# Attention and gated convolution on one core: key loads of later batches over 17 to 22 groups, later expected landings and a new set of order weights

## The chip, the cores and the metric

The kernel runs on one core of a Trainium2 chip. A time is device microseconds (us) from start to end of one execution of the program. The core has a matrix engine (PE, with its weight loads shown apart as PEld), a vector engine (DVE), a scalar engine (ACT), a general engine (POOL) and a queue engine (SP), which here issues every DMA: loads, stores and DMA transposes. Each engine works through its own instructions strictly in the order in which they stand in the program, and waits for semaphores of the others.

## The reference, cut to what matters

```python
# B, C, Hh, Ww = 4, 128, 384, 32;  N = Hh * Ww = 12288 queries a batch;  r = 4
kv_pool = kv.reshape(B, H // r, r, W // r, r, C).mean(axis=(2, 4))
k = v = kv_pool.reshape(B, -1, C) @ w_sr             # 768 keys a batch
s = (q @ k.transpose(0, 2, 1)) / np.sqrt(C)
a = np.exp(s - s.max(-1, keepdims=True))
a /= a.sum(-1, keepdims=True) + 1e-09
x = a @ v                                            # (B, 12288, 128)
gate_pre[t] = sum(conv_w[k] * x[t - 4 + k] for k in range(5))
gate = 1.0 / (1.0 + np.exp(-gate_pre))
out = (gate * (x @ w_val)) @ w_out
```

## The kernel before, in words

**Tiles.** Queries are worked in groups of 512 (98 groups over all four batches: 24 each, the last 512 queries in three smaller ones). A group has four parts j of 128 queries. For each part PE makes scores (line 527: six matmuls into one of three PSUM buffers `s`), DVE takes the row maximum (`nm`, line 539), ACT the exponential (line 546), DVE the factor one over the row sum (`r`, lines 555 and 560), ACT writes the scaled rows as the high half in f16 (`hl`, line 574), DVE the low half (`hl`, line 585), which also gives the PSUM buffer back. Two parts share one `hl` buffer, and when both are written SP turns them with one DMA transpose (`pt`, line 598). So a group has two transposes; below they are called its first and its second. When both have landed PE multiplies them with the values (`av`, line 669, 18 matmuls), ACT copies the result to `x`, POOL works the five taps of the gate (lines 730 and 738), and PE, DVE and ACT do the two projections (lines 757, 761, 766, 771). Every second group SP loads `q` for two groups (512 KB, line 499) and stores `out` for two groups (512 KB, line 794).

**Keys.** The keys and values of a batch come from 16 pieces of `in_kv` of 384 KB each. SP loads a piece into one of six buffers `kvt` (line 283), and DVE sums it in two halves into `pool` (`TENSOR_REDUCE`, line 301). When all 16 are summed PE projects them (line 354), ACT and DVE split them into high and low, and PE makes the values (line 447). The pieces of batch 0 come at the start of the program. Those of batch 1, 2 and 3 are loaded and summed while the groups of the batch ahead run.

**What sets the order.** Nothing here is ordered by hand. The code first adds all steps to a `Plan` with an engine, an assumed duration, a due time and what they follow; `Plan.order` then runs a list scheduler over them with buffers, and the instructions are written out in the order that it finds. The due times of the steps are the group's place times `PERIOD` plus an offset from the table `DUE`; among the steps that an engine can begin within `WAIT` of the first one the scheduler takes the one that is due first. For a DMA it keeps a queue of its own, in which a transfer lands `DMA_LEAD`, its duration and `DMA_TAIL` after its issue, and `CLUMP` pulls copies together. These assumed times change only the order of instructions. Each engine then waits for real events on the chip.

The loads of the later batches have a first time, rounded up to every second group by `grid`:

```python
at = (lambda i: 0.0) if first else (lambda i: grid((b * NG - 22 + i // 2 * 2) * T))
s = plan.add("SP", 1.0 if first else 1.3, due(-20 * T + i) if first else at(i), run,
             takes=(buf,), start=at(i))
```

So piece 0 and 1 are meant for one stretch of two groups, piece 2 and 3 for the next, and so on: two pieces for every two groups, over 16 groups, from 22 groups ahead of the batch to 6 ahead of it. Below, two groups with their loads are called a slot.

Of the kernel before, what the change touches and what calls it, by code (L numbers as in the profile page):

```python
# [19 lines left out]
PIECES = 16  # L20
PARTS = 2

PERIOD = 10.07
DUE = dict(keys=-41.48, vals=-22.35, vals0=16.98, q=-57.56, qh=-1.25, ql=-98.01,
           score=(-8.15, -7.91, -7.36, -6.79), max=(-32.5, -0.27, -16.2, -12.23),
           exp=(5.15, -44.96, 24.96, -21.92), hi=(-25.76, -32.45, 4.7, -5.26),
           lo=(20.43, -7.54, 6.54, -13.12), turn=(-0.19, 7.8, 7.04, -30.79), pe=-16.02, thi=48.8,
           tlo=0.37, r=(-26.97, -87.57, -32.65, -35.38), grid=-0.27, av=20.43, avs=3.47,
           halo=41.12, x=41.54, gate=30.15, th=62.39, val=46.47, h=-8.22, out=4.34, evac=7.73,
           store=61.44, end_diag=-62.42, end_gate=17.3, end_th=63.48, end_val=94.9, end_h=-18.98,  # L30
           end_out=45.64, end_evac=-44.23)


class Step:
# [8 lines left out]
class Plan:  # L43
# [2 lines left out]

    EDGE = 0.04
    LAG = dict(PE=0.16, ACT=0.1, DVE=0.085, POOL=0.04, SP=0.0)
    WAIT = dict(PE=0.08, ACT=0.2, DVE=0.11, POOL=0.01, SP=0.59)
    DMA_LEAD, DMA_TAIL, CLUMP = 1.3, 0.8, 39.63  # L50

    def __init__(self):
        self.steps, self.stock = [], {}
# [14 lines left out]
    def order(self):  # L68
# [10 lines left out]
        dma = 0.0  # L79
        until, placed = {}, []  # L80
        while any(ready.values()):
            best = None
            for e, items in ready.items():
# [8 lines left out]
                if not ests:  # L92
                    continue
                t0 = min(t for t, _ in ests)
                s = min((s.due - (s.kind == last[e] == "copy") * self.CLUMP, n, s)
                        for n, (t, s) in enumerate(ests) if t <= t0 + self.WAIT[e])[2]
# [4 lines left out]
            t, e, s = best  # L101
# [6 lines left out]
            if e == "SP":  # L108
                copy = s.kind == "copy"
                free[e] = t + (0.5 if copy else s.dur)  # L110
                switch = 1.0 if last[e] == "copy" and not copy else 0.0
                dma = max(dma + switch, t + self.DMA_LEAD) + s.dur
                s.end = dma + self.DMA_TAIL
            else:
                free[e] = t + s.dur
                s.end = t + s.dur + s.lag
# [33 lines left out]
def attn_moe_kernel(ctx, tc, qT, kvT, w_sr, w_moe, outT):  # L150
# [9 lines left out]
    NG = N // GQ  # L160
# [3 lines left out]
    T = PERIOD  # L164
# [100 lines left out]
    def grid(t):  # L265
        return D["grid"] + 2 * T * -(-(t - D["grid"]) // (2 * T))

    def setup(b, st):

        first = b == 0  # L270
        due = (lambda at: at - 40.0) if first else (lambda at: b * NG * T + at)
        at = (lambda i: 0.0) if first else (lambda i: grid((b * NG - 22 + i // 2 * 2) * T))
        sums = {}
        holder = {}

        def load(i):
            buf = "o" if first and i in SPARE else "kvt"
            cuts = (0, PC * RR // 2, PC * RR) if first and i == PIECES - 1 else (0, PC * RR)

            def run():  # L280
                s.tile = tile_of(s, buf)
                for c0, c1 in zip(cuts, cuts[1:]):
                    nc.sync.dma_start(out=s.tile[:, c0:c1], in_=kvT[b, i, :, c0:c1])  # L283
            s = plan.add("SP", 1.0 if first else 1.3, due(-20 * T + i) if first else at(i), run,
                         takes=(buf,), start=at(i))
            return s, buf

        def pool_of(s, k0):
# [194 lines left out]
    def group(g, prev, nxt):  # L483
# [9 lines left out]
        if off == 0 or g.i == 1:  # L493
            cols = GQ if g.i < 2 else 2 * GQ

            def load():
                if off == 0:
# [2 lines left out]
                                  in_=qT[g.b, :, g.c0:g.c0 + cols])  # L500
            at = FIRST_Q[g.i] if g.i in FIRST_Q else grid(t0 + D["q"])
            ld = plan.add("SP", 1.6 * cols / (2 * GQ), at, load, [ld],
                          takes=("q",) if off == 0 else (), start=at)
            if off == 0:
                g.io.ld = ld

# [59 lines left out]
        def straight(j, sc, r):  # L566
# [28 lines left out]
            def turn():  # L595
                if g.pt_by is s_t:
# [4 lines left out]
            s_t = plan.add("SP", 1.40 * width, t0 + j * T / 4 + D["turn"][j], turn,  # L601
                           [s_lo] if alone else [s_lo, g.los[j - 1]],
                           takes=() if g.pt_by else ("pt",),
                           frees=[(g.hl_by, "hl")], kind="turn")
            owner(s_t)
            g.ready.append(s_t)

# [245 lines left out]

ON_PE, IN_S = 2, 4
TAIL, LAST, LAST_TURNED = 4, (2, 1, 1), ((), (0,), (0,))
FIRST_VALS = 26.0
FIRST_Q = {0: 17.0, 1: 17.5, 2: 18.0, 4: 26.0}
SPARE, FOLDED = (6, 7, 8), (3, 5, 8, 10, 12)
TURNED = ((),)
# [28 lines left out]
```

## Time and profile before

| | us |
|---|---|
| median of 3 runs | 1046.62 |
| lowest and highest of them | 1041.93 and 1050.76 |
| the profiled execution | 1049.91 |
| its span, first to last instruction | 1048.0 |
| PE busy in it | 1001.0 |
| DVE, ACT, POOL busy in it | 929.9, 886.2, 931.3 |
| mean granted clock of PE | 0.987 of full |

The profiled execution is 3.3 us above the median and lies 1.9 us above its own span. A span of 1048.0 us over 98 groups mixes three kinds of time: the start, before the first groups run, stretches in which keys of the next batch are loaded beside the groups, and stretches without key loads. They have to be read apart.

### The profile page before, as it was taken

Reading aid. Unit: us, or ns where it says so; the run is one execution under the profiler, and the core shown is the slowest. Engines: PE = TensorE matmul, PEld = TensorE weight load, DVE = VectorE, ACT = ScalarE, POOL = GpSimd, SP = SyncE. Lnnn points to the kernel's source line nnn. Section 1 sums busy time; section 2 is a strip of 40 time slices with the busy share of each in tenths; the row PEclk is TensorE's granted clock in tenths of the full one; section 3 lists DMA queues with packets and bytes.
Section 4 is the critical chain, followed back from the end, with each engine's and each line's share of the span. In section 5 each row is a group of like instructions: output and inputs, shape, how many; then the busy total and the mean of one; then the engine's idle time right before and its main releaser. Section 6 shows DMA issues by size and latency. Waiting matters only on the chain.

```text
span 1048.0 us, 15461 instructions
## 1 busy us (share of the span) xinstructions
PE 1001.0 (96%) x4586; PEld 612.0 (58%) x4586; DVE 929.9 (89%) x1806; ACT 886.2 (85%) x1584; POOL 931.3 (89%) x1069
## 2 busy tenths in 40 slices
PE   4789999999999999999999999999999999999998
PEld 3555555556665555556666555555566666666655
DVE  6799989989899998989989999899998988988884
ACT  1688878889888888879998888798999899989884
POOL 5179989998999988989899999899999999999994
PEclk9799999999999999999999999999999999999999
DMA  8599999999999999999999999999999999999983
GB/s 313 135 220 231 222 220 242 235 226 209 218 213 226 228 236 248 214 225 208 217 209 218 249 242 222 230 236 220 224 214 197 222 201 217 214 202 212 191 171 91
DMA packets 616994, 227.05 MB, mean 217 GB/s; under 512 B 595536, under 2 KB 596304, under 8 KB 616912
## 3 DMA queue, kind: packets, MB, share of 16 engines
q1 hardware_dynamic: 616912, 226.07, 102.4%
q8 instruction: 37, 0.61, 0.2%
q14 instruction: 45, 0.37, 0.1%
HBM read 50.66 MB, written 25.17 MB: 72 GB/s over the span
## 4 chain that ended last, share of the span: by engine, by line
PE 82%; DMA 9%; DVE 6%; SPq 1%; issue 1%; ACT 1%; POOL 0%; ACTq 0%
PE s L527 35%; PE av L669 31%; PE m L757 7%; PE m L766 7%; DMA kvt<-in_kv 4%; DMA pt<-hl 4%; DVE hl L585 3%; DVE nm L539 2%; DVE pool L301 1%; DMA o<-in_kv 1%; SPq L598 1%; ACT hl L574 0%; PE m L354 0%; SPq L283 0%; PE m L447 0%
## 5 line engine op out<-in xcount | busy, mean ns | idle before, releaser
L738 POOL TENSOR_TENSOR gate<-gate,tap 128x512 f32<-128x512 f32 x376 | 482.2, 1282 | 9.8
L585 DVE SCALAR_TENSOR_TENSOR hl<-s,r,hl 128x768 f16<-128x768 f32 x382 | 386.1, 1013 | 38.0 <-ACT hl L574 37.5
L669 PE MATMUL av<-pt,vh 128*128 128x512 f16 (+2 forms) x1176 | 385.8, 379 | 3.1 <-DMA pt<-hl 3.1
L546 ACT ACTIVATE s<-s,nm 128x768 f32<-128x768 f32 x384 | 336.6, 877 | 55.3 <-DVE nm L539 54.6
L539 DVE TENSOR_REDUCE nm<-s 128x1 f32<-128x768 f32 x384 | 362.8, 946 | 14.4 <-PE s L527 13.9
L574 ACT ACTIVATE hl<-s,r 128x768 f16<-128x768 f32 x382 | 338.3, 906 | 41.7 <-DVE r L560 36.5
L527 PE MATMUL s<-kh,qh 128*128 128x512 f32 (+1 forms) x768 | 267.5, 429 | 26.2 <-DVE r L555 17.2
L730 POOL TENSOR_SCALAR tap<-x,wb 128x512 f32<-128x512 f32 x376 | 254.5, 698 | 0.0
L669 PE MATMUL av<-pt,vl 128*128 128x512 f16 (+2 forms) x588 | 222.2, 378 | 0.0
L527 PEld LDWEIGHTS s<-kh,qh 128*128 128x128 f32 x768 | 135.1, 191 | 144.3 <-issue 59.9
L669 PEld LDWEIGHTS <-vh 128*128 128x128 f16 x1176 | 113.8, 98 | 154.2 <-issue 59.9
L527 PE MATMUL s<-kl,qh 128*128 128x512 f32 (+1 forms) x768 | 199.9, 342 | 0.0
L527 PE MATMUL s<-kh,ql 128*128 128x512 f32 (+1 forms) x768 | 199.2, 341 | 0.0
L513 POOL TENSOR_TENSOR ql<-q,qh 128x512 fp32r<-128x512 f32 (+1 forms) x98 | 123.2, 1257 | 24.5 <-ACT qh L509 24.5
L527 PEld LDWEIGHTS s<-kh,ql 128*128 128x128 f32 x768 | 120.0, 192 | 17.3
L527 PEld LDWEIGHTS s<-kl,qh 128*128 128x128 f32 x768 | 119.6, 191 | 17.6 <-DVE kl L394 0.2
L730 POOL TENSOR_SCALAR gate<-x,wb 128x512 f32<-128x512 f32 x94 | 65.5, 697 | 59.4 <-ACT x L687 58.4
L766 PE MATMUL m<-h,wm 128*128 128x512 f32 x188 | 100.4, 616 | 0.0
L757 PE MATMUL m<-x,wb 128*128 128x512 f32 x188 | 96.0, 592 | 0.0
L669 PEld LDWEIGHTS <-vl 128*128 128x128 f16 x588 | 58.3, 99 | 62.0 <-issue 24.4
L301 DVE TENSOR_REDUCE pool<-kvt 128x24 f32<-128x384 f32 x114 | 60.4, 540 | 21.8 <-DMA kvt<-in_kv 21.8
L771 ACT ACTIVATE o<-m 128x512 f32<-128x512 f32 x94 | 56.3, 599 | 23.0 <-PE m L766 22.3
(67 smaller groups left out, 622.8 us busy)
## 6 DMA issues: line engine op xcount, KB each, us to landing
q<-in_q SPq DMA_DIRECT2D x47, 512.0 KB, 5.6
out<-o SPq DMA_DIRECT2D x47, 512.0 KB, 3.3
kvt<-in_kv SPq DMA_DIRECT2D x60, 384.0 KB, 4.3
pt<-hl SPq DMA_TRANSPOSE x191, 6.3
o<-in_kv SPq DMA_DIRECT2D x3, 384.0 KB, 8.0
q<-in_q SPq DMA_DIRECT2D x2, 256.0 KB, 5.2
kvt<-in_kv SPq DMA_DIRECT2D x2, 192.0 KB, 4.5
raw<-in_w_moe SPq DMA_DIRECT2D x1, 261.0 KB, 2.9
```

The costliest lines, as they stand in the source:

```text
L301: v.tensor_reduce(out=dst, in_=src[:, part * n:][:, :n], axis=AX.X, op=ALU.add)
L513: nc.gpsimd.tensor_tensor(out=g.ql, in0=g.io.q[:, mine], in1=g.qh.bitcast(F32), op=ALU.subtract)
L527: nc.tensor.matmul(t[:, c0:c1], a[:, sl], k[:, c0:c1], start=(i == 0), stop=(i == 2))
L539: v.tensor_reduce(out=s.tile, in_=sc.tile[:, :NK], axis=AX.X, op=ALU.max, negate=True)
L546: nc.scalar.activation(out=sc.tile[:, :NK], in_=sc.tile[:, :NK], func=AF.Exp, bias=mx.tile, accum_out=sc.tile[:, NK:NK + 1])
L574: nc.scalar.activation(out=g.hls[j // 2][:, half, 0], in_=sc.tile[:, :NK], func=AF.Copy, scale=r.tile)
L585: v.scalar_tensor_tensor(out=hl[:, half, 1], in0=sc.tile[:, :NK], scalar=r.tile, in1=hl[:, half, 0], op0=ALU.mult, op1=ALU.subtract)
L669: nc.tensor.matmul(g.av, st[name][:, k * P:(k + 1) * P], g.pt[:, :, a * NCH + k], start=(i == 0), stop=(i == len(AV) - 1))
L730: nc.gpsimd.tensor_scalar(out=s.tile, in0=src(k), scalar1=wt(k), scalar2=1.0, op0=ALU.mult, op1=ALU.mult)
L738: nc.gpsimd.tensor_tensor(out=g.gate, in0=g.gate, in1=tap.tile, op=ALU.add)
L757: nc.tensor.matmul(g.m, st["wb"][:, :C], g.x[:, HALO:], start=True, stop=True)
L766: nc.tensor.matmul(g.m2, wout, g.h, start=True, stop=True)
```

## The change

It does four things, all in the planner's input. The pieces of a later batch get first times spread evenly from 27 groups ahead of the batch (22 for batch 1, whose pieces cannot be asked for before the program begins) up to `KEYS_BY`, 5 groups ahead of it. The scheduler adds `SLACK` to the assumed landing of a key load (2.0 us), a query load (0.5 us) and a transpose (0.1 us). `PERIOD` and the whole table `DUE` have other numbers, of which two lines are shown. `WAIT` and `CLUMP` have other numbers. No instruction is added, removed or resized; the first lines of the file grow, so that a line of the kernel before has a number higher by 6 to 8 after (283 becomes 289, 301 becomes 307, 598 becomes 605).

```diff
-PERIOD = 10.07
-DUE = dict(keys=-41.48, vals=-22.35, vals0=16.98, q=-57.56, qh=-1.25, ql=-98.01,
+PERIOD = 9.97
+DUE = dict(keys=-39.58, vals=-35.42, vals0=17.37, q=-44.21, qh=4.86, ql=-80.97,
...
+SLACK = dict(keys=2.0, q=0.5, turn=0.1)
...
-    WAIT = dict(PE=0.08, ACT=0.2, DVE=0.11, POOL=0.01, SP=0.59)
-    DMA_LEAD, DMA_TAIL, CLUMP = 1.3, 0.8, 39.63
+    WAIT = dict(PE=0.07, ACT=0.26, DVE=0.12, POOL=0.07, SP=0.8)
+    DMA_LEAD, DMA_TAIL, CLUMP = 1.3, 0.8, 16.23
...
-                s.end = dma + self.DMA_TAIL
+                s.end = dma + self.DMA_TAIL + s.lag
...
-        at = (lambda i: 0.0) if first else (lambda i: grid((b * NG - 22 + i // 2 * 2) * T))
+        lo = -22 if b == 1 else -27
+        at = (lambda i: 0.0) if first else (
+            lambda i: grid((b * NG + lo + (KEYS_BY - lo) * i / PIECES) * T))
...
-                         takes=(buf,), start=at(i))
+                         takes=(buf,), start=at(i), lag=0.0 if first else SLACK["keys"])
...
+                          lag=0.0 if g.i in FIRST_Q else SLACK["q"])
...
+                           lag=SLACK["turn"])
...
-FIRST_VALS = 26.0
+FIRST_VALS, KEYS_BY = 26.0, -5
```

What this does to the order shows best on the queue of SP. Here is a stretch of it in the middle of batch 1, before, while the pieces of batch 2 come in. `kvt` is a key piece, `q` a query load, `out` a store, and a `DMA_TRANSPOSE` is half a group; two transposes with one `pt` are one group:

```order
L598 DMA_TRANSPOSE pt_4058<-hl_3974 128x24x128
L283 DMA kvt_4092<-in_kv 128x768
L283 DMA kvt_4096<-in_kv 128x768
L499 DMA q_4109<-in_q 128x1024
L598 DMA_TRANSPOSE pt_4058<-hl_4052 128x24x128
L794 DMA out<-o_3996 128x1024
L598 DMA_TRANSPOSE pt_4172<-hl_4131 128x24x128
L598 DMA_TRANSPOSE pt_4172<-hl_4185 128x24x128
L598 DMA_TRANSPOSE pt_4322<-hl_4225 128x24x128
L283 DMA kvt_4353<-in_kv 128x768
L283 DMA kvt_4360<-in_kv 128x768
L499 DMA q_4374<-in_q 128x1024
```

And the same stretch after:

```order
L605 DMA_TRANSPOSE pt_4196<-hl_4137 128x24x128
L802 DMA out<-o_4010 128x1024
L289 DMA kvt_4240<-in_kv 128x768
L505 DMA q_4255<-in_q 128x1024
L605 DMA_TRANSPOSE pt_4196<-hl_4191 128x24x128
L605 DMA_TRANSPOSE pt_4318<-hl_4234 128x24x128
L605 DMA_TRANSPOSE pt_4318<-hl_4313 128x24x128
L605 DMA_TRANSPOSE pt_4436<-hl_4383 128x24x128
L802 DMA out<-o_4257 128x1024
L289 DMA kvt_4485<-in_kv 128x768
L289 DMA kvt_4500<-in_kv 128x768
L505 DMA q_4507<-in_q 128x1024
```

A slot now holds one piece or two: for batch 2 and for batch 3 five slots of two and six of one, eleven in all, where there were eight of two. For batch 1 seven slots of two remain, and the last two pieces stand in slots of their own. The store now stands ahead of the pieces and of the group's second transpose; before it stood behind that transpose.

On DVE the first sum of a piece moves. Before, in the same batch, the sum of piece 6 (`kvt_4092`) stands between the two low halves of the next group's first transpose, with 14 instructions between it and the low half that the transpose ahead of the loads waits for:

```order
L539 TENSOR_REDUCE nm_4127<-s_4102 128x1
L555 SCALAR_TENSOR_TENSOR r_4136<-s_4080,unit 128x1
L560 RECIPROCAL r_4140<-r_4136 128x1
L585 SCALAR_TENSOR_TENSOR hl_4131<-s_4063,r_4124,hl_4131 128x768
L301 TENSOR_REDUCE pool_3412<-kvt_4092 128x24
L585 SCALAR_TENSOR_TENSOR hl_4131<-s_4080,r_4140,hl_4131 128x768
L555 SCALAR_TENSOR_TENSOR r_4170<-s_4102,unit 128x1
```

After, the sum of piece 10 (`kvt_4240`) stands half a group later, with 24 instructions between it and that low half (`hl_4137`):

```order
L592 SCALAR_TENSOR_TENSOR hl_4234<-s_4221,r_4286,hl_4234 128x768
L562 SCALAR_TENSOR_TENSOR r_4316<-s_4272,unit 128x1
L567 RECIPROCAL r_4327<-r_4316 128x1
L307 TENSOR_REDUCE pool_2794<-kvt_4240 128x24
L592 SCALAR_TENSOR_TENSOR hl_4313<-s_4248,r_4303,hl_4313 128x768
L546 TENSOR_REDUCE nm_4338<-s_4320 128x1
L592 SCALAR_TENSOR_TENSOR hl_4313<-s_4272,r_4327,hl_4313 128x768
```

At the start SP's queue begins with the loads of `q` for the first groups (`q_179` is groups 0 and 1, in two halves). Before:

```order
L499 DMA q_179<-in_q 128x512
L499 DMA q_186<-in_q 128x1024
L499 DMA q_179<-in_q 128x512
L499 DMA q_210<-in_q 128x1024
L499 DMA q_258<-in_q 128x1024
L598 DMA_TRANSPOSE pt_280<-hl_260 128x24x128
L598 DMA_TRANSPOSE pt_280<-hl_296 128x24x128
L283 DMA kvt_374<-in_kv 128x768
L283 DMA kvt_379<-in_kv 128x768
L499 DMA q_392<-in_q 128x1024
L598 DMA_TRANSPOSE pt_412<-hl_361 128x24x128
L598 DMA_TRANSPOSE pt_412<-hl_400 128x24x128
```

After, the second half of `q_179` stands behind one more load, and the first transpose of group 2 (`pt_366`) stands ahead of both transposes of group 1 (`pt_422`):

```order
L505 DMA q_179<-in_q 128x512
L505 DMA q_186<-in_q 128x1024
L505 DMA q_196<-in_q 128x1024
L505 DMA q_179<-in_q 128x512
L505 DMA q_258<-in_q 128x1024
L605 DMA_TRANSPOSE pt_280<-hl_260 128x24x128
L605 DMA_TRANSPOSE pt_280<-hl_292 128x24x128
L605 DMA_TRANSPOSE pt_366<-hl_325 128x24x128
L289 DMA kvt_396<-in_kv 128x768
L289 DMA kvt_398<-in_kv 128x768
L505 DMA q_412<-in_q 128x1024
L605 DMA_TRANSPOSE pt_422<-hl_388 128x24x128
```

From the middle of batch 3 on, where no keys are left to load, PE, DVE, ACT and POOL hold the same order as before within a group, but for one `av` matmul that PE takes ahead of a score instead of behind it; on SP the query load stands one or two transposes earlier.

## Rows read from the trace of the kernel before

**Rows 1.** The page's first part: busy us of each engine, share of the span, instructions.

```profile
PE 1001.0 (96%) x4586; PEld 612.0 (58%) x4586; DVE 929.9 (89%) x1806; ACT 886.2 (85%) x1584; POOL 931.3 (89%) x1069
```

**Rows 2.** Busy time by stretch. Columns: the stretch and its length, then busy us (and instructions) of PE, PEld, DVE, ACT and POOL, the granted clock, the share of the DMA engines, GB/s. The stretches are the start; the rest of batch 0, in which the keys of batch 1 come in; batch 1, with the keys of batch 2; batch 2, with those of batch 3; batch 3 up to its last groups, without key loads.

```profile
0.00:60.00 60.00, 37.60 (x148) 28.36 (x148) 43.43 (x93) 28.72 (x52) 20.52 (x37) 0.89 0.76 221
60.00:275.00 215.00, 207.27 (x952) 124.53 (x952) 198.01 (x386) 187.66 (x337) 198.30 (x227) 0.99 1.09 226
275.00:531.00 256.00, 248.19 (x1125) 148.90 (x1124) 231.31 (x452) 221.13 (x395) 234.66 (x265) 0.99 1.08 222
531.00:781.00 250.00, 244.53 (x1119) 147.35 (x1119) 229.86 (x447) 220.45 (x394) 233.20 (x265) 0.99 1.09 228
781.00:1010.00 229.00, 229.00 (x1058) 141.79 (x1057) 204.49 (x391) 207.44 (x370) 221.92 (x251) 1.00 1.01 205
```

**Rows 3.** The same view for four short stretches in which the granted clock fell.

```profile
136.00:146.00 10.00, 7.89 (x29) 3.96 (x27) 6.81 (x14) 6.01 (x12) 7.07 (x8) 0.83 1.13 266
408.00:420.00 12.00, 9.79 (x38) 5.36 (x36) 7.72 (x16) 7.53 (x13) 8.24 (x10) 0.86 1.15 260
452.00:464.00 12.00, 9.89 (x38) 5.24 (x37) 7.79 (x16) 7.62 (x14) 8.63 (x11) 0.86 1.11 255
661.00:672.00 11.00, 8.56 (x35) 5.17 (x33) 6.62 (x15) 6.87 (x13) 6.15 (x6) 0.84 1.07 271
```

**Rows 4.** Pieces of the chain that ended last, in order of time: start us, us, what. The first three lie in batch 1 while keys are loaded, the last two in batch 3.

```profile
320.98 4.13 DMA kvt<-in_kv
...
344.30 10.03 DMA pt<-hl
...
406.67 4.29 DMA kvt<-in_kv
...
830.09 1.31 PE av L669 x6
...
909.91 1.31 PE av L669 x6
```

**Rows 5.** DVE's instructions in order of time in one slot of batch 1: start us, us, engine, line, operation; in brackets idle time before it and what ended it.

```profile
357.50 1.00 DVE L585 SCALAR_TENSOR_TENSOR hl<-s,r,hl 128x768 f16<-128x768 f32 x1
...
362.90 0.68 DVE L761 SCALAR_TENSOR_TENSOR h<-th,m 128x512 f32<-128x512 f32 x1
363.49 0.15 DVE L555 SCALAR_TENSOR_TENSOR r<-s,unit 128x1 f32<-128x1 f32 x1
...
363.75 0.94 DVE L539 TENSOR_REDUCE nm<-s 128x1 f32<-128x768 f32 x1
...
364.88 1.02 DVE L585 SCALAR_TENSOR_TENSOR hl<-s,r,hl 128x768 f16<-128x768 f32 x1
368.06 0.55 DVE L301 TENSOR_REDUCE pool<-kvt 128x24 f32<-128x384 f32 x1 [2.17 <-DMA kvt<-in_kv]
```

**Rows 6.** The sums of key pieces (line 301) by stretch, 62 to 275, 275 to 531 and 531 to 781 us. For the first the group with its durations in ns; then for each what DVE waited for ahead of them: us in all, times.

```profile
L301 DVE TENSOR_REDUCE pool<-kvt x29: 531/534/553, 62.5 to 213.0; 128x24 f32<-128x384 f32 x29
...
  DMA kvt<-in_kv: 4.8, 4
...
  DMA kvt<-in_kv: 8.5, 5
...
  DMA kvt<-in_kv: 5.7, 4
```

**Rows 7.** SP's instructions in order of time in one slot of batch 1. For a row of several the us run from the first one's start to the last one's end.

```profile
364.05 1.06 SPq L283 DMA_DIRECT2D kvt<-in_kv  x2
...
365.69 6.52 SPq L598 DMA_TRANSPOSE pt<-hl  x1
372.30 0.53 SPq L794 DMA_DIRECT2D out<-o  x1
372.93 12.42 SPq L598 DMA_TRANSPOSE pt<-hl  x3
385.40 1.05 SPq L283 DMA_DIRECT2D kvt<-in_kv  x2
```

**Rows 8.** The same in batch 3, without key loads.

```profile
801.25 13.28 SPq L598 DMA_TRANSPOSE pt<-hl  x3
814.58 0.58 SPq L794 DMA_DIRECT2D out<-o  x1
815.54 9.02 SPq L598 DMA_TRANSPOSE pt<-hl  x2
824.66 0.53 SPq L499 DMA_DIRECT2D q<-in_q  x1
```

**Rows 9.** Transposes on SP by stretch, issue durations in ns (least, median, most), and us from issue to landing (the same three): the one that stands behind two pieces at 344.3 us, then 780 to 1005 us.

```profile
DMA to landing us min/median/max: 10.0/10.0/10.0
...
L598 SPq DMA_TRANSPOSE pt<-hl x45: 3073/4074/4887, 781.0 to 1000.6; - x45
...
DMA to landing us min/median/max: 4.6/6.3/7.9
```

**Rows 10.** PE's first `av` matmul of group 74, in order of time.

```profile
828.22 0.38 PE L669 MATMUL av<-pt,vh 128*128 128x512 f16 x1
```

**Rows 11.** Two instructions of the start in order of time: ACT's copy of the second half of `q_179`, and PE's first `av` matmul of group 1.

```profile
33.45 0.62 ACT L509 CAST qh<-q 128x512 fp32r<-128x512 f32 x1 [1.59 <-issue]
...
60.41 0.38 PE L669 MATMUL av<-pt,vh 128*128 128x512 f16 x1 [0.35 <-DMA pt<-hl]
```

More of the change, by code (lines that the diff above doesn't have):

```diff
@@ L21 @@
 PARTS = 2
-PERIOD = 10.07
-DUE = dict(keys=-41.48, vals=-22.35, vals0=16.98, q=-57.56, qh=-1.25, ql=-98.01,
[L25 to L31, printed above, removed]
+PERIOD = 9.97
+DUE = dict(keys=-39.58, vals=-35.42, vals0=17.37, q=-44.21, qh=4.86, ql=-80.97,
+           score=(-7.47, -6.32, -5.63, -6.47), max=(-23.77, -6.1, 13.1, -11.57),
+           exp=(0.09, -30.82, -8.74, -13.77), hi=(-29.44, -20.58, 0.7, -43.56),
+           lo=(22.34, -32.12, 5.51, 24.31), turn=(-11.32, 15.47, 2.1, 15.6), pe=6.0, thi=29.07,
+           tlo=-11.13, r=(-50.81, -28.34, -47.73, -28.55), grid=-1.12, av=20.41, avs=4.86,
+           halo=63.51, x=42.45, gate=30.41, th=53.25, val=47.33, h=-3.27, out=11.86, evac=21.59,
+           store=52.32, end_diag=-56.57, end_gate=26.44, end_th=54.36, end_val=54.8, end_h=-26.7,
+           end_out=56.32, end_evac=-38.92)
+SLACK = dict(keys=2.0, q=0.5, turn=0.1)
 class Step:
@@ L502, in group @@
             ld = plan.add("SP", 1.6 * cols / (2 * GQ), at, load, [ld],
-                          takes=("q",) if off == 0 else (), start=at)
+                          takes=("q",) if off == 0 else (), start=at,
+                          lag=0.0 if g.i in FIRST_Q else SLACK["q"])
             if off == 0:
@@ L603, in straight @@
                            takes=() if g.pt_by else ("pt",),
-                           frees=[(g.hl_by, "hl")], kind="turn")
+                           frees=[(g.hl_by, "hl")], kind="turn",
+                           lag=SLACK["turn"])
             owner(s_t)
```

## The prediction

> **What bounds the kernel now.** I read the busy times first, then the stretches, then the chain, then the two queues that it names. The page has PE at 96% [rows 1], which alone says little about where time can still come from. The stretches say it [rows 2]: in batch 3, where no keys are loaded, PE is busy for 229.00 of 229 us, so nothing on another engine can shorten that part while PE's work stays what it is. In the three stretches with key loads PE is idle for 7.73, 7.81 and 5.47 us (length less busy), 21.0 in all, and in 22.4 us of the start. Besides, the granted clock drops to its half level (1.2 instead of 2.4 GHz) for short times, each where PE has just waited [rows 3]: (1 - 0.83) x 10, (1 - 0.86) x 12 twice and (1 - 0.84) x 11 us make 1.7 each, one in the first stretch, two in the second, one in the third. So what a perfect schedule of the key loads could give back is 7.7 + 1.7 = 9.4, 7.8 + 3.4 = 11.2 and 5.5 + 1.7 = 7.2 us, 27.8 together. The change removes no work, so its ceiling is this and a few us of the start.
>
> The chain agrees in pace. From 320.98 to 406.67 us, eight groups with two pieces a slot, it takes 85.7 us; from 830.09 to 909.91, eight groups without, 79.8 [rows 4]. That is 1.5 us for a slot of two groups.
>
> Two things hold a slot back, and they are tied to each other. First, **DVE waits for a key piece**. In the slot shown, DVE ends the low half that the transpose ahead of the loads needs at 358.50 and comes to the first sum after its other work, but the piece has landed only at 368.06: DVE stands for 2.17 us [rows 5], and with it the low half behind the sum, which frees a score buffer for PE. This happens 13 times, 4.8 + 8.5 + 5.7 = 19.0 us of DVE [rows 6], about PE's idle time. Second, **SP's queue is full**. From one pair of pieces to the next it is occupied from 364.05 to 385.40 with gaps of 0.1 us at most, 21.35 us for two groups [rows 7], where PE needs 19.96 (a quarter of 79.8). Without key loads the same queue has four transposes of 4.07, a query load of 0.53 and a store of 0.58 [rows 8, 9], 17.4 us of 19.96. So two pieces cost it 3.95 us, one about 2.0 (an estimate, half of the pair): a slot of one piece needs 19.4 and fits under PE with 0.56 to spare, a slot of two is 1.39 over.
>
> **The change, part by part.** It moves instructions only, so each part is a wait that goes or comes.
>
> *Fewer pieces in a slot, batches 2 and 3.* Eight slots of two become five of two and six of one. SP's queue is over by 5 x 1.39 = 7.0 us and has 6 x 0.56 = 3.4 to spare between, so at most some 3.6 us of backlog arises in a batch instead of 8 x 1.39 = 11.1. A backlog reaches PE only when it eats the cushion between a transpose's landing and its `av`: the second transpose of group 74 is issued at 815.54 [rows 8], `av` begins at 828.22 [rows 10], and landing takes 6.3 [rows 9], which leaves 6.4. DVE, too, gets under PE: without keys it is busy for 204.49 of 229 us [rows 2], 8.91 a group of 9.98; two sums of 0.534 [rows 6] on every group, as before, make 9.98, no spare at all, and 16 pieces over 22 groups make 8.91 + 0.78 = 9.69. POOL has 221.92 of 229 and is not touched.
>
> *The sum expected later.* Before, 14 instructions cover the loads: three low halves of 1.00, three maxima of 0.94, one `h` of 0.68, six small ones of 0.15 and one sum of 0.53 [rows 5, 6] make 7.9 us, where 368.06 - 358.50 = 9.6 were needed. After, 24 instructions make 12.2 (four, five, one, twelve and two of them). Counted so over all slots of batches 2 and 3 the cover is 10.0 to 12.4 us or more, against 9.6 and 0.6 for the store that is now issued ahead. The waits of 8.5 and 5.7 us should go nearly all, and with them the score buffers held up and the falls of the clock behind them. What is late next is PE's own work, as in batch 3.
>
> I take 9 of the 11.2 us in batch 1's stretch and 5.5 of the 7.2 in batch 2's. The ends are nothing and all.
>
> *Batch 1's keys.* Seven slots of two remain, and each is still 1.39 over on SP. Only the sum moves, from 8 us of cover or so to between 10.3 and 14.1 in the slots behind the first two. The 4.8 us of waits should go; the queue stays full. Of 9.4 us I take 3.5, less than half, between nothing and 9.4.
>
> *Query loads and stores moved.* The store ahead of the second transpose waits for ACT's evacuation of `out`, and the query load for POOL to have used up its buffer. In the trace of before both are done before the new place in the queue is reached in all but four early slots, where SP would wait for the store a little. I put it at nothing; what covers it is the transposes' cushion of 6.4 us.
>
> *The start.* Here the order of PE and DVE changes. ACT's copy of the second half of `q_179` held ACT for 1.59 us before [rows 11] and now stands behind the next exponential, so group 0 gains that. Against it, two transposes of group 1 stand behind one of group 2, 4.07 us more in the queue, and `av` of group 1 already waited for its transposes by 0.35 [rows 11]; PE has two more scores ahead of the first `av` to fill the time with. I take a gain of 1 us, between a loss of 5 and a gain of 5. The key projections' work on PE is the same, and so is the tail but for swaps of a few matmuls: nothing, with 1 us either way.
>
> The sum: 9 + 5.5 + 3.5 + 1 = 19 us off the profiled execution's 1049.91, which is 1030.9. That execution lies 3.3 us above the median, 1046.62; taken off the median the same gain would give 1027.6. Some of the runs' spread is waits and clock falls that the change should take away, so I stay nearer to the first: **1030 us**.
>
> **The rivals.**
>
> *A. The queue stays the bound.* A transpose behind two pieces lands 10.0 us after its issue against 6.3 [rows 9], and the chain runs through such a landing at 344.30 [rows 4]. After, the store of 512 KB stands ahead of it as well. If slots of two still cost their 1.39 us, with no credit from slots of one, then 6 in the first stretch behind the start and 5 in each of the others leave 22 us of what before cost 27.8; the gain is 6 and 1 for the start, 1043. For it: SP has no gap in the slot shown. Against it: the cushion of 6.4 us is larger than one slot's excess, and slots of one now stand between.
> The Trainium skill (DMA: Bandwidth & Descriptors, section Queues, rings and completion order) says that on each DMA engine descriptors are consumed in ring order. By that the transpose would wait out the store as well, some 2.5 us at the 205 GB/s of the last stretch, and land 12.5 us after its issue, 0.2 before its `av` wants it; the sum by the skill is then this rival's. No row of before has a store in that place.
>
> *B. Everything goes.* PE idles nowhere between 60 us and the tail, and the clock holds: 1049.9 - 27.8 - 1 = 1021.
>
> *C. The start loses.* Group 1's transposes land a place later, `av` of group 1 waits 4.07 more, and the gain elsewhere holds: 1030.9 + 1 + 4 = 1036.
>
> *D. Slower.* The mechanism is the clump on SP: store, one or two pieces and query load in one go ahead of a group's second transpose, in eleven slots for each of batches 2 and 3 and nine for batch 1 instead of eight, eight and eight. If the transpose behind it lands so late that `av` waits in every slot, single or not, then from 27.8 / 31 = 0.9 us a slot the change loses. With 1.2 us a slot the time is 1049.9 - 27.8 + 37.2 = 1059. Against it: a slot of one piece moves less ahead of that transpose than a pair did without a store, 384 + 512 KB against 768, and before, pairs did not make `av` wait that long.
>
> *E. It does nothing.* The order does change as the text says, with seven pairs left for batch 1 alone, so this would need DVE's waits to have cost PE nothing; but the chain runs through the landing of a key piece again and again [rows 4], so I give it little: 1047.
>
> **How the numbers follow.** I give the forecast with its ends (1024 to 1036) 0.57, A 0.17, B 0.10, C 0.06, D 0.06 and E 0.04. The range of 8 in 10 runs from B's 1021 to A's 1043; outside it lie D, E and a part of B. A measurement of this kernel tells about 1% from no change, so faster means under 1036.2: the forecast, B and half of C and a little of A, 0.71. Within 1% are most of A, E and the rest of C, 0.23. Slower is D, 0.06.
>
> **What would show it.** Right: no sum of a key piece that waits for its load by more than half a us in batches 1 and 2; PE idle in those two stretches under 3 us each; no half-clock stretch there; the eight-group pace in batch 1 at 80 to 81 us instead of 85.7; SP with gaps in slots of one piece. The first stretch is still slower than batch 3 by some us, with SP full. Wrong: `av` waiting for `pt` in every slot of two, or transposes landing 12 us after their issue (A, D); a first `av` of group 1 later than 62 us with PE idle ahead of it (C); waits of DVE for key pieces that remain, in the slots with 10.0 us of cover first.

## The result and the profile after

| | before | after |
|---|---|---|
| median of 6 runs, us | 1046.07 | 1021.9 |
| lowest and highest | 1041.93 and 1050.76 | 1019.04 and 1022.28 |
| profiled execution and its span | 1049.91, 1048.0 | 1022.09, 1020.2 |

The ratio is 0.976, with a 95% interval of 0.9728 to 0.9793: 2.4% faster, where 1030 us (1.6%) was forecast. In the profiled executions the gain is 27.8 us, as much as the prediction had called the ceiling; that execution of the kernel before lies above its median, and between the medians the gain is 24.2 us.

The busy times, and the stretches as in [rows 1, 2], cut at the same places in the work:

```profile
PE 991.6 (97%) x4586; PEld 606.9 (59%) x4586; DVE 930.5 (91%) x1806; ACT 884.9 (87%) x1584; POOL 930.6 (91%) x1069
```

```profile
0.00:60.00 60.00, 37.89 (x151) 28.86 (x152) 45.21 (x94) 30.04 (x54) 20.65 (x37) 0.91 0.81 232
60.00:275.00 215.00, 211.83 (x978) 127.36 (x978) 205.29 (x401) 191.27 (x343) 203.13 (x231) 1.00 1.09 236
275.00:520.00 245.00, 244.94 (x1132) 147.95 (x1131) 232.83 (x455) 222.15 (x397) 236.34 (x268) 1.00 1.09 235
520.00:765.00 245.00, 244.82 (x1135) 148.40 (x1133) 230.14 (x447) 223.55 (x402) 237.16 (x269) 1.00 1.08 229
765.00:985.00 220.00, 220.00 (x1017) 134.30 (x1016) 196.36 (x376) 198.30 (x354) 213.20 (x244) 1.00 1.03 204
```

PE is idle for 3.17, 0.06 and 0.18 us in the three stretches with key loads, where it was 7.73, 7.81 and 5.47, and the granted clock stays full behind the start. What PE and DVE wait for, over the whole span (us in all, times, longest), and DVE's same wait before:

```profile
PE m L360 <- DVE pool L307: 10.3, 4, 9.1
PE s L534 <- DVE hl L592: 8.1, 7, 3.2
PE m L360 <- POOL pool L326: 3.6, 4, 1.5
PE s L534 <- DVE r L562: 2.5, 3, 1.2
PE av L677 <- ACT s L553: 0.5, 1, 0.5
...
DVE pool L307 <- DMA kvt<-in_kv: 2.8, 3, 1.0
```

```profile
DVE pool L301 <- DMA kvt<-in_kv: 21.8, 16, 2.7
```

DVE's 21.8 us for key pieces are 2.8, all of them in the start: of the 19.0 us in the three stretches [rows 6] nothing is left. All but 3.1 us of PE's waits up there lie in the first 60 us. PE waits for a transposed tile once more, at 61.15 us, where group 1's first `av` stands for 0.46 us. The view puts that wait down to ACT, but the ACT step that this `av` waits for in the program, the copy of group 0's result to `x`, had ended at 58.2, and the transpose that it needs was issued at 55.76 and landed 5.3 us later, at 61.02:

```profile
57.60 0.60 ACT L695 ACTIVATE x<-av 128x512 f32<-128x512 f32 x1 [0.51 <-PE av L677]
...
L605 SPq DMA_TRANSPOSE pt<-hl x1: 3348/3348/3348, 55.8 to 55.8; - x1
...
DMA to landing us min/median/max: 5.3/5.3/5.3
...
61.15 0.38 PE L677 MATMUL av<-pt,vh 128*128 128x512 f16 x1 [0.46 <-ACT s L553]
```

SP's queue in the same part of batch 1 as [rows 7]:

```profile
363.91 0.57 SPq L802 DMA_DIRECT2D out<-o  x1
364.53 0.42 SPq L289 DMA_DIRECT2D kvt<-in_kv  x1
365.05 0.87 SPq L505 DMA_DIRECT2D q<-in_q  x1
366.02 16.85 SPq L605 DMA_TRANSPOSE pt<-hl  x4
382.92 0.57 SPq L802 DMA_DIRECT2D out<-o  x1
383.55 1.37 SPq L289 DMA_DIRECT2D kvt<-in_kv  x2
385.02 0.43 SPq L505 DMA_DIRECT2D q<-in_q  x1
385.55 17.58 SPq L605 DMA_TRANSPOSE pt<-hl  x4
403.19 0.57 SPq L802 DMA_DIRECT2D out<-o  x1
```

The slot of one piece takes 19.01 us and the one of two 20.27, where the prediction had 19.4 and 21.35. Other slots of two in which SP has no gap to speak of take 19.8 to 21.3. The queue of transposes over batch 1's stretch, 275 to 520 us, before and then after (ns least, median, most; landing):

```profile
L598 SPq DMA_TRANSPOSE pt<-hl x46: 3507/4188/7264, 275.3 to 515.4; - x46
...
DMA to landing us min/median/max: 5.5/6.5/10.0
```

```profile
L605 SPq DMA_TRANSPOSE pt<-hl x49: 2835/3813/6132, 275.0 to 516.8; - x49
...
DMA to landing us min/median/max: 4.5/6.1/9.0
```

The transposes themselves have become shorter, the least by 0.67 us and the median by 0.38, though the same bytes are moved by the same instruction. No term of the prediction has that, and the last four experiments show why.

### The profile page after: what moved, and what is told of

It is laid out like the page before. It is cut to its first block, busy times and chain, and to the rows that moved or that the text cites. A ratio compares the mean times of both kernels' runs of the same rounds, so it can differ in the third digit from the quotient of the medians.

```text
span 1020.2 us, 15459 instructions
## 1 busy us (share of the span) xinstructions
PE 991.6 (97%) x4586; PEld 606.9 (59%) x4586; DVE 930.5 (91%) x1806; ACT 884.9 (87%) x1584; POOL 930.6 (91%) x1069
## 4 chain that ended last, share of the span: by engine, by line
PE 78%; POOL 5%; DVE 2%; ACT 1%; issue 0%; POOLq 0%; ACTq 0%; DVEq 0%
PE s L534 33%; PE av L677 30%; PE m L774 7%; PE m L765 7%; POOL gate L746 2%; POOL tap L738 1%; DVE hl L592 1%; POOL ql L520 1%; ACT hl L581 0%; DVE nm L546 0%; POOL gate L738 0%; PE m L453 0%; PE m L360 0%; ACT s L553 0%; PE s L824 0%
## 5 line engine op out<-in xcount | busy, mean ns | idle before, releaser
L677 PE MATMUL av<-pt,vh 128*128 128x512 f16 (+2 forms) x1176 | 370.8, 377 | 0.5 <-ACT s L553 0.5
L534 PE MATMUL s<-kh,qh 128*128 128x512 f32 (+1 forms) x768 | 261.0, 421 | 11.0 <-DVE hl L592 8.1
L534 PEld LDWEIGHTS s<-kh,qh 128*128 128x128 f32 x768 | 132.2, 191 | 130.2 <-issue 54.9
L677 PEld LDWEIGHTS <-vh 128*128 128x128 f16 x1176 | 107.5, 98 | 142.6 <-issue 55.4
L567 DVE RECIPROCAL r<-r 128x1 f32<-128x1 f32 x384 | 62.9, 164 | 13.1
```

The source lines that it names most:

```text
L534: nc.tensor.matmul(t[:, c0:c1], a[:, sl], k[:, c0:c1], start=(i == 0), stop=(i == 2))
L567: v.reciprocal(out=s.tile, in_=e.tile)
L677: nc.tensor.matmul(g.av, st[name][:, k * P:(k + 1) * P], g.pt[:, :, a * NCH + k], start=(i == 0), stop=(i == len(AV) - 1))
```

## The experiments

Times are medians; the kernel before, run beside each set of experiments, gave 1047 to 1049. The intervals are those of the ratio to it. Code cuts are shortened: the loops around them are left out.

### The parts, one at a time

Theory 1: DVE's waits for key pieces cost the time. Theory 2: the queue does. **e1** moves the sums alone, in the order that the planner has made:

```
-    for step in plan.order():
+    placed = plan.order()
+    for b in range(1, B):
+        for i in range(0, PIECES, 2):
+            first, second = ...   # first half-sum of piece i, of piece i + 1
+            placed.remove(first)
+            placed.insert(placed.index(second), first)
+    for step in placed:
```

> The kernel before, with its own order on every engine but for one move: of each pair of key pieces the first half-sum of the first piece stands on DVE directly ahead of that of the second, 2 to 3 us of DVE's work later. SP's queue, the pairs, the weights stay. Theory 1 (the time was DVE standing for a piece that had not landed, nothing else): the cover rises from 7.4 to 10.2 us to between 9.7 and 12.8, the 19 us of waits on kvt fall under 4, PE's idle time in the three key stretches falls from 21 to under 6, half-clock stretches after the start go: 1022 to 1028. Rival (SP's queue is over by 1.39 us for every slot of two pieces, and the waits were only where that shows): 1038 to 1046, with PE waiting for transposes instead.

Measured: 1044.5, 0.9959 [0.9936, 0.9982]. The waits went from the sums to the transposes:

```profile
PE av L670 <- DMA pt<-hl: 9.7, 11, 1.5
```

```profile
DVE pool L301 <- DMA kvt<-in_kv: 8.5, 13, 1.3
```

SP's queue has hardly a gap in batch 1's slots with keys, and from group 26 to 40 a slot takes it 21.4 us on the mean. Theory 1 falls: a cover of DVE work is no use while the queue is behind.

**e2, e3, e4** take one part of the diff each: the lags (`SLACK` and its three uses), the 17 and 22 groups (`lo`, `KEYS_BY`), and the numbers (`PERIOD`, `DUE`, `WAIT`, `CLUMP`).

> The kernel before with SLACK alone: key loads, query loads and transposes are expected to land later by 2.0, 0.5 and 0.1 us; loads in pairs over 16 groups and the order weights of before. By the order, nearly every first sum has 10.2 us of cover or more. Theory 1: 1022 to 1027, most of the change. Rival (the queue): eight pairs a batch remain, 1038 to 1044. Second rival (the new order weights carry the gain): 1040 to 1047.

> The kernel before with the new first times of key loads alone (17 and 22 groups, one or two pieces a slot), no SLACK, order weights of before. By the order, batch 0 is as before with 8 us of cover, and batch 1 keeps six sums at 7.4 us. Theory 1: batch 0 loses as before, batch 1 about half, batch 2 little: 1032 to 1040. Rival (the queue): five pairs a batch instead of eight take away the excess: 1027 to 1033.

> The kernel before with the new PERIOD, DUE, WAIT and CLUMP alone: loads in pairs over 16 groups, no SLACK. By the order about half of the first sums have 7.4 to 9 us of cover and the rest 9.7 or more. Theory 1: 1032 to 1040, with waits on kvt of about 10 us. Rival (the queue, pairs): 1042 to 1047. If the weights alone carry the gain: 1022 to 1028.

Measured: 1040.2 (0.9912 [0.9873, 0.9951]), 1044.2 (0.9951 [0.9919, 0.9983]), 1037.2 (0.9873 [0.9826, 0.9921]). The three gains add up to 25 us, about the whole change: no part carries it, and the fewer pieces in a slot, which the prediction named first, give least alone. As tests of the two theories they do not agree: e2 lies where theory 2 had it, e4 where theory 1 had it, and e3 above both ranges. None of them is clean. What is found further below, that a transpose from buffer `hl0` is shorter, changes in each: `hl0` stands behind another transpose or a store 6 times in the kernel before (and in e1, e5, e6, e9 and e10), 37 times in e2, 25 in e3, 44 in e4 and 47 in the changed kernel. How much of each gain is the part and how much the buffer no run here shows.

### What stands where on SP's queue

In the kernel before the transpose behind a lone store issues in 4.6 us where one behind a transpose takes 3.7 (medians); the changed kernel has the store together with the loads. Theory 3: that place is it. **e5** moves the store there in the kernel before, **e6** does so in e1, **e7** takes it out again in the changed kernel. **e8** is the changed kernel without the longer loading.

```
+    # e5, e6: each store to directly ahead of the next pair of key loads on SP
+    placed.remove(store); placed.insert(placed.index(key), store)
+    # e7: each store ahead of key loads to behind the next transpose
+    placed.remove(store); placed.insert(placed.index(turn) + 1, store)
```

> The kernel before, in which each store of the output (of the stretches with key loads) is moved on SP's queue alone from its place between two transposes to directly ahead of the next pair of key pieces, so that the queue goes from copies to transposes once per slot of two groups instead of twice. Nothing else moves. Theory 'the store's place': the transpose behind a lone store takes 4.5 us to issue (356 to 361 and 373 to 378 in the trace of before) where one behind a transpose takes 3.6 to 3.7; with the store in the clump the queue's slot falls from 21.4 by about 1 us towards PE's 20.0, and most of the 19 us for which DVE waits for key tiles goes: 1035 to 1040. Rival 'the place of the store is nothing, the sums and the order of the other engines did it': 1044 to 1049, the waits for key tiles at 16 to 20 us as before.

> As e5_store_in_clump, and each pair's first half-sum moved directly ahead of the second piece's first half-sum on DVE, as in e1_sums_later (1044.5 there). Theory 'the store's place': e1 failed because SP's queue was too slow for the pairs, so that the wait went from the sums to the transposes; with the queue at PE's pace both waits go: 1024 to 1032, and less than e1 and e5 by more than 6 us each. Rival: 1041 to 1045, as e1, with PE's wait for transposed tiles at 8 to 10 us.

> The changed kernel, in which each store that stands at the head of a clump of key loads is moved on SP's queue behind the first transpose after that clump: twice from copies to transposes per slot, as before. Nothing else moves. Theory 'the store's place': the slots of two pieces fall behind PE again, 1028 to 1036, with waits for key tiles or transposed tiles of 5 to 12 us. Rival: 1021 to 1024.

> The changed kernel without the longer loading: the slack and the new weights, but pairs of key pieces over 16 groups as before (every slot of two groups loads two pieces; most stores stand in the clump, as in the changed kernel). Theory 'the store's place and the sums' cover': the longer loading is not needed, 1021 to 1026, and the slots of two pieces run at PE's pace (39.9 to 40.2 us for four groups outside the key work). Rival 'the three parts add up' (2.3 us of e3 alone to 4.6): 1026 to 1028. Rival 'fewer pieces per slot is what lets the queue keep up', as the prediction had it: 1035 to 1041.

Measured: e5 1067.5 (1.0186 [1.0154, 1.0219]), e6 1048.2 (1.0016 [0.9995, 1.0037]), e7 1022.6 (0.9763 [0.9736, 0.9789]), e8 1030.9 (0.9844 [0.9821, 0.9867]). Theory 3 falls on both sides: e5 is slower than either range had it, e6 too, and e7 loses nothing. In e5 the pieces land later by the store ahead of them, and DVE has no cover for that:

```profile
DVE pool L302 <- DMA kvt<-in_kv: 34.3, 18, 3.7
```

e8 lies between its ranges. It shows that the longer loading is worth 8 to 9 us on top of the rest, but also that slots of two pieces need about 20.3 us of SP in this order, not 21.35 (PE needs 19.97). The loss is not spread over the slots. In batch 1's stretch, with eight slots of two, e8 loses 1.3 us against the changed kernel, and in batch 2's 6.9 (by the ends of `av`). Most of that is one place, where a transpose behind two pieces landed 10.8 us after its issue; PE stood for it, and the granted clock of the 40 us around it was 0.96:

```profile
622.04 0.39 PE L675 MATMUL av<-pt,vh 128*128 128x512 f16 x1 [4.03 <-DMA pt<-hl]
```

**e9** and **e10** move the keys on SP alone, in the kernel before, by two transposes and by a whole slot; **e11** moves them in the changed kernel back to between an odd group's transposes, where before has them.

```
+    for pair in pairs:               # of key loads on SP's queue
+        turn = transposes_ahead(pair)[-2]     # e9, e11; e10: the query load ahead
+        placed.remove(pair); placed.insert(placed.index(turn), pair)
```

> The kernel before, in which each pair of key pieces of the later batches is moved on SP's queue two transposes earlier: from between the two transposes of an odd group to between those of the even group ahead of it, where the changed kernel has most of its key loads (in batch 1's stretch right behind the store). The query load stays where it was, and nothing moves on any other engine. Theory 'place': the transposes move their data faster with the keys there (in the trace after, the even group's first transpose, ahead of the clump, takes 2.9 us of data time, in the one before 3.8), and the keys land some 9 us before their sum: both waits go, 1022 to 1032. Theory 'fixed demand', on which the prediction's shares rest: SP's queue needs 21.4 us per slot wherever the keys stand, so that the waits for key tiles turn into waits for transposed tiles, as in e1_sums_later: 1038 to 1046.

> The kernel before, in which each pair of key pieces of the later batches is moved on SP's queue one whole slot (two groups, four transposes) earlier, to the head of the clump ahead of it: the queue looks as before, with the keys between the two transposes of an odd group, and the keys land 20 us earlier against their sums. Nothing else moves. Theory 'place' and theory 'fixed demand' alike: the waits for key tiles go but the queue stays at 21 to 22 us per slot, and PE waits for transposed tiles: 1038 to 1046, as e1_sums_later. Theory 'lateness alone' (keys that land early are enough, and the queue gives way): 1022 to 1032.

> The changed kernel, in which the key pieces of the later batches are moved on SP's queue two transposes earlier, to between the two transposes of an odd group, where the kernel before has them; the store and the query load stay, nothing else moves, and the keys land some 8 us earlier still. Theory 'place': the queue's slots of two pieces need more than PE's 20.0 us again, 1030 to 1042, with waits for transposed tiles of 5 us and more. Theories 'fixed demand' and 'lateness alone': 1021 to 1026.

Measured: 1041.2 (0.9941 [0.9919, 0.9962]), 1040.6 (0.9925 [0.9897, 0.9953]), 1022.5 (0.977 [0.9728, 0.9813]). The place falls too. In e9 and e10 the keys are early enough (DVE waits for them 2.8 and 2.9 us in all), and PE waits for transposes, in e9:

```profile
PE av L670 <- DMA pt<-hl: 18.6, 13, 2.7
```

So SP's queue was the bound before, whatever stood where on it, and in the changed kernel it is not, whatever stands where on it.

### The buffer that a transpose reads from

The packets of the transposes (the pieces in which the DMA engines move them, 3072 of 256 bytes each) show what differs. A transpose moves its data in about 2.95 us or in about 3.8. The moved GB/s in 40 slices, in the kernel before from 357.8 to 365.3 us, two transposes one behind the other, and after from 362.0 to 364.9, one:

```profile
GB/s 89 220 221 217 220 210 224 214 218 216 224 213 218 218 220 212 224 210 179 138 193 235 221 218 210 199 227 221 213 212 221 224 213 213 221 224 214 213 203 231
```

```profile
GB/s 106 215 272 286 297 282 297 282 290 293 293 290 290 286 293 286 297 290 286 297 286 293 286 286 300 286 290 290 297 282 268 265 286 268 300 293 297 248 128 57
```

217 GB/s and 290. What tells them apart is not the place alone; it is which of the four buffers `hl` is read. In the 13 kernels up to here, of the transposes that stand behind another transpose, 176 of 206 from `hl0` took under 3.4 us from the first packet to the last, and 21 of 1173 from the other three. By rate (the median over twelve equal pieces of a transpose) all 206 from `hl0` are over 255 GB/s, and 215 of the 1173, of which 197 had slowed to under 150 GB/s in one piece. `hl0` alone starts at a multiple of 256 bytes in its partition (96000); the others begin 64 to 192 bytes behind one. Behind the loads most reach the fast rate from any buffer: 197 of 280 from the other three, in their second half, when the loads are out. In the kernel before, `hl0` falls in the key stretches to the odd group's second transpose, which stands behind the loads, and most there would be fast anyway. The new order takes the buffers in another turn: `hl0` falls to the even group's first transpose, behind another one. Four experiments on that, with no instruction moved:

```
-        return where.tile(shape, dt, name=f"{name}{step.slot[name]}")
+        return where.tile(shape, dt, name=f"{name}{step.slot[name]}",
+                          align_bytes=256 if name in ("hl",) else None)
```

is **e12** on the kernel before, **e13** on the changed one and **e15** on e1. **e14** takes `hl0` off its place in the changed kernel:

```
+        if name == "hl" and not step.slot[name]:
+            wide = where.tile([P, 4 * NK + 16], dt, name="hl0", align_bytes=256)
+            return wide[:, 16:].rearrange("p (a b k) -> p a b k", a=2, b=2)
```

> The kernel before with the four buffers hl, from which SP's transposes read, each at a start address that is a multiple of 256 bytes within the partition (before: hl0 alone). No instruction moves. Theory 'source address': the transposes behind another transpose or a store issue in 2.9 to 3.3 us instead of 3.65 to 3.8, SP's slot of two pieces falls from 21.4 to 19.0 to 19.5 us, below PE's 20.0, the keys are issued earlier and most of the waits for key tiles go: 1022 to 1034. Theory 'the rate follows the order, the buffer is chance': 1044 to 1049, transposes at 3.65 to 3.8.

> The changed kernel with the four buffers hl at multiples of 256 bytes. Theory 'source address': all transposes fast, SP's queue idle for 2 us and more in each slot, but PE is the bound (it waits 0.4 us in the three stretches with key loads behind the start's), so 1018 to 1022. Theory 'order': 1021 to 1023, transposes as they are.

> The changed kernel with buffer hl0 moved 32 bytes off its multiple of 256 (the other three are off in it anyway). No instruction moves. Theory 'source address': the even group's first transpose takes 3.8 us of data time instead of 3.2, a slot of two pieces needs 20.8 to 21.2 us and one of one piece 19.5, on the mean a little over PE's 20.0; batch 0's slots, two pieces each, fall behind most: 1024 to 1033. Theory 'order': 1021 to 1023.

> e1_sums_later (the kernel before, first half-sum of each pair moved back on DVE; 1044.5) with the four buffers hl at multiples of 256 bytes. Theory 'source address': the sums no longer wait and the transposes no longer are late: 1020 to 1027, near the changed kernel, with none of its three parts. Theory 'order': 1042 to 1046.

Measured: e12 1025.3 (0.9792 [0.9757, 0.9826]), e13 1022.0 (0.9745 [0.972, 0.977]), e14 1029.9 (0.9827 [0.98, 0.9853]), e15 1026.2 (0.9789 [0.9767, 0.9811]). e12, e14 and e15 lie where the theory of the source address has them, and outside the other theory's ranges; e13 cannot tell, since both had 1022. The transposes of 275 to 520 us, in e12 and in e14:

```profile
L599 SPq DMA_TRANSPOSE pt<-hl x49: 2881/3231/7307, 272.1 to 515.4; - x49
...
DMA to landing us min/median/max: 4.5/5.6/9.5
```

```profile
L608 SPq DMA_TRANSPOSE pt<-hl x49: 3587/4022/7281, 272.5 to 519.0; - x49
...
DMA to landing us min/median/max: 5.4/6.3/10.6
```

From the packets, transposes behind another transpose, median us from a transpose's first packet to its last, with the buffer's distance behind a multiple of 256 bytes:

| | hl0 | hl1 | hl2 | hl3 |
|---|---|---|---|---|
| before (`hl0`: five of them, none in the key stretches) | 0: 3.00 | 160: 3.83 | 64: 3.83 | 192: 3.81 |
| e12 | 0: 2.95 | 0: 2.98 | 0: 3.05 | 0: 2.98 |
| after | 0: 3.01 | 128: 3.80 | 96: 3.82 | 192: 3.81 |
| e14 | 32: 3.78 | 96: 3.81 | 64: 3.81 | 160: 3.81 |

Where the data goes to does not tell the two prices apart: with a destination 64 bytes behind a multiple of 256 the medians are 2.98 in e12 and 3.83 in e14.

In e12 SP has gaps in nearly every slot, DVE waits for keys 4.9 us instead of 21.8, and PE is idle for 2.53, 0.42 and 1.23 us in the three stretches:

```profile
60.00:275.00 215.00, 212.47 (x985) 128.99 (x986) 205.03 (x402) 194.28 (x349) 205.27 (x234) 1.00 1.03 233
275.00:520.00 245.00, 244.58 (x1130) 148.20 (x1129) 231.33 (x450) 221.99 (x395) 235.06 (x267) 1.00 1.03 233
520.00:765.00 245.00, 243.77 (x1127) 147.24 (x1125) 231.05 (x452) 222.58 (x400) 234.43 (x267) 1.00 1.04 233
```

One argument to a buffer's allocation gives 22.6 us without the change, which gives 24 to 26; on top of it the change is worth 3.3 us (e13 against e12). In e14 PE is idle for 2.92 and 2.69 us in batches 1 and 2 instead of 0.06 and 0.18, and waits for transposes again (6.9 us, 9 times):

```profile
275.00:520.00 245.00, 242.08 (x1119) 146.06 (x1117) 229.82 (x448) 218.99 (x392) 232.81 (x265) 1.00 1.12 232
520.00:765.00 245.00, 242.31 (x1118) 146.49 (x1118) 228.16 (x443) 220.43 (x396) 233.65 (x265) 1.00 1.10 227
```

The two slots that were shown of the changed kernel, in e14, take 19.78 and 20.83 us instead of 19.01 and 20.27:

```profile
367.74 0.58 SPq L805 DMA_DIRECT2D out<-o  x1
368.37 0.43 SPq L292 DMA_DIRECT2D kvt<-in_kv  x1
...
387.52 0.57 SPq L805 DMA_DIRECT2D out<-o  x1
388.15 1.30 SPq L292 DMA_DIRECT2D kvt<-in_kv  x2
...
408.35 0.57 SPq L805 DMA_DIRECT2D out<-o  x1
```

No version beats the changed kernel by more than its runs scatter: e13's 1022.0 against 1021.9. In batch 1's stretch PE is busy for at least 244.9 of 245 us in both.

## Why the prediction was right in direction and too small

Gains by stretch in the profiled executions, from the ends of `av` of groups 7, 24, 48 and 72, beside the terms of the sum:

| us | forecast | e14, hl0 off | after |
|---|---|---|---|
| start | 1 | 1.0 | 1.4 |
| batch 1's keys | 3.5 | 2.6 | 4.8 |
| batch 1's stretch | 9 | 9.7 | 12.6 |
| batch 2's stretch | 5.5 | 5.2 | 8.0 |
| sum | 19 | 18.5 | 26.9 |

The cut between the first two rows is not the forecast's, which was at 60 us: there the gain is 0.1 in e14 and 0.5 after, and 3.5 and 5.8 go to batch 1's keys.

- **The step that failed** is the price of SP's slot. The prediction read "21.35 us for two groups" and "four transposes of 4.07" off the trace and took both as fixed by the number of copies. A transpose has two prices here, 2.95 and 3.8 us of data, by the buffer that it reads, and the change of order handed the one fast buffer to another transpose. That makes one transpose of each slot 0.8 us shorter; without it (e14) the two slots shown are 0.77 and 0.56 us longer, and the run takes 1029.9 us instead of 1021.9. With it a slot of one piece has about 1 us of spare instead of 0.56, a slot of two is 0.3 over instead of 1.39, and the shares taken (9 of 11.2, 5.5 of 7.2, 3.5 of 9.4) become all, but for 3 us in the first stretch, where PE waits for DVE and once for a transpose.
- **The mechanism was right, and the sum too, at the old price**: e14, the same instructions with every source off, gave 1029.9 us, and each term within 1 us. That is closer than single executions can show, since those of the kernel before lie up to 8.8 us apart; to that extent it is luck. Two steps on the way were not right even there. A slot of one piece was put at 19.4 us, with half of a pair's price, and the one shown takes 19.78; a slot of two was put at 21.35 and the one shown takes 20.83, so that the two errors nearly cancel. And the cushion of 6.4 us was to keep `av` from waiting for transposes, where in e14 it waits 9 times, 6.9 us in all.
- **What bounds the kernel** was read right: about the ceiling is what came. That both numbers are 27.8 is luck, since the gain holds 1.4 us of the start and 0.9 of the tail. Part of it shows as PE's busy time, 991.6 against 1001.0, with the falls of the clock behind the start gone (mean granted clock 0.995, before 0.987). The two things that hold a slot back are one: the sums waited because the queue was late. e12 leaves every sum in its place and the waits fall from 21.8 to 4.9 us; e9 and e10 bring the keys early and leave the queue late, and get 6 to 7 us.
- **Fewer pieces in a slot** is worth 8 to 9 us once the queue is close to PE's pace (e8 against the changed kernel), but not slot by slot, as the prediction counts it: eight slots of two in batch 1 cost 1.3 us, and one late transpose in batch 2 most of the rest. Why that one was so late stays open. Alone (e3) it gives 4.6.
- **Query loads and stores moved**: nothing, as put, for the stores (e7); the query loads were not moved by themselves.
- **Rivals.** B's 1021 came out, by something that B did not name. A is out: the Trainium skill (DMA: Bandwidth & Descriptors, section Queues, rings and completion order), as the prediction applied it, had a transpose behind store and pieces land 12.5 us after its issue; the longest landing of the whole run is 9.7. C is out: the first `av` of group 1 does wait for its transpose, but for 0.46 us at 61.15, about as before (0.35), and not for 4.07 more. D is out: no later `av` waits for a transpose. E is out.
- Of what was to show it: sums that wait, PE idle, clock and pace (79.9 us for eight groups in batch 1) came as said, and SP has gaps in most slots of one piece, though not in the one shown. "The first stretch is still slower, with SP full" came in small: PE is idle there for 3.17 us, but SP is full in some of its slots alone, and seven groups from group 9 on take 70.0 us, PE's own pace.

Left open: whether the 8 us between e8 and the changed kernel remain with all sources aligned, how much of e2, e3 and e4 is the buffer, and the 3.3 us between e12 and e13, which were not taken apart. The slots' gaps in e12 say that SP is not the bound there.

## What to carry to other kernels

When a queue is the bound, split the duration of its instructions by buffer as well as by place before you take it as a price: two modes in one group (2.8 to 6.1 us with a median of 3.8) are a question, not scatter. When a reordering gains more or less than its terms add up to, look at which buffer each instruction now gets, since a planner that hands out buffers changes addresses together with the order. And a source of DMA transposes is best allocated at a multiple of 256 bytes: here that alone did nine tenths of what a retuned schedule did.

## What the runs showed of the hardware

- A DMA transpose of 768 KB behind another one moves its data at 290 GB/s from a source that starts at a multiple of 256 bytes in its partition, and at 217 from one that starts 32, 64, 96, 128, 160 or 192 bytes behind one. The destinations were off such a multiple in every kernel, and their distance does not tell the two rates apart (64 bytes: 2.98 us in e12, 3.83 in e14). The Trainium skill (DMA: Bandwidth & Descriptors, section How a descriptor splits into AXI transactions) says that a read that doesn't start at a multiple of 256 bytes is split so that a first transaction fetches unused bytes. The runs agree in direction; whether these fetches are the cause no run here shows.
- It is not only the address. In the 13 kernels ahead of e12, 197 of 280 transposes from off buffers that stand behind the loads reached the fast rate in their second half; behind a store it was 85 of 347. And behind a stop of some tenths of a us a transpose from an off buffer was fast too. After, from 354.0 to 361.4 us, the rate goes from 217 over a stop to 290 within one transpose of `hl3`:

```profile
GB/s 217 206 206 212 226 219 216 209 219 224 219 214 213 221 223 213 214 199 126 147 228 231 210 196 256 208 194 57 11 7 11 275 289 291 288 289 289 292 292 291
```

  Why the fast mode begins with a stop and is lost again, often by the next transpose, stays open.
